# Sliding-window attention beside a gated feed-forward, one core: both heads of a pair in the two partition halves

## The chip, the cores and the metric

One core of one Trainium2 chip runs the kernel. The metric is the device time of an execution in microseconds (us), as the median of several executions; "span" is the length of the one execution that the profiler recorded, which is 1.6 to 1.8 us shorter than the time.

## The reference

The kernel computes one transformer layer: attention and a gated feed-forward from the same normalised input.

```python
# x: 1 x 2048 x 512;  32 heads of 16;  F = 1792
xn = layernorm(x)
q, k, v = split_heads(xn @ wqkv)
scores = q @ k.T * 16 ** -0.5            # per head
mask = (i - j >= 0) & (i - j < 256)      # causal, window of 256
o = softmax(where(mask, scores, -1e9)) @ v
out = x + o @ wo + ((xn @ w_gate) * (xn @ w_up)) @ w_down
```

## The kernel before

The 2048 tokens are four chunks (T) of 512 queries. The 32 heads are 16 pairs per token: a quarter c of the model's columns holds eight heads, four "even" ones (par 0) and four "odd" ones (par 1), and each of the four sits in its own block of 32 partitions (e). So there are 4 x 4 = 16 "pairs" (T, c), each of two "heads" (par) that really are four heads side by side. A head of 16 needs only a part of the matrix engine's 128 x 128 array, so the attention's matmuls are small tiles, and they are placed between the full-array matmuls of the feed-forward and the projections ("fillers"), whose order the program fixes beforehand.

A bank is here one 128 x 512 float32 tile of the memory that the matrix engine writes to: S has four, and four more (tag M) serve everything else in turn. In the profile's lines gp and up are the feed-forward's gate and up, psd is the sum of down and wo, acc that of the values, and OT the transposed attention output.

Scores come in batches of one four-bank tile S, one exponential each. The keys are on the partitions of the result. In the kernel before, an EVEN or ODD batch is of one par and puts the two 64-key halves of a key block into the two partition halves; a PLAIN batch holds what is left of both:

```python
def scores(self, T, c, kind, par):                      # 76 batches in all
    S = self.ps_s.tile([128, 4, 512], F32, tag="S")     # the one score tile
    for p, kb, h, q, n, col in self.score_pieces(T, kind, par):
        ...                                             # keys of one half, or of a block
        for e in range(4):
            nc.tensor.matmul(S[outs, e, col:col + n], lhsT=(Ko if p else K)[U][rows, c, keys],
                             rhs=Q[T][rows, c, q:q + n], tile_position=(32 * e, outs.start), ...)
    P = self.ppool.tile([128, 4, 512], BF16, tag="P")
    nc.scalar.activation(out=P[:], in_=S[:], func=ACT.Exp, scale=0.25)
    ...                                                 # POOL masks; DVE masks later
```

The value products contract over all 128 partitions. Where only one 64-key half of a block counts, they use copies of V with the other half zero (Vu, Vl), so half of the rows multiply zeros:

```python
def values(self, T, c, par):                            # 64 matmuls per head
    acc = self.ps_m.tile([128, 512], F32, tag="M")      # one of four banks, shared with the fillers
    for i, (P, col, h, kb, q, n) in enumerate(todo):
        V = self.V[U] if h == 2 else self.Vh[U % 2][h]  # whole, upper half or lower half
        for e in range(4):
            nc.tensor.matmul(acc[32 * e:32 * e + 32, q:q + n], lhsT=V[:, at:at + 32],
                             rhs=P[:, e, col:col + n], tile_position=(0, 32 * e), ...)
    nc.vector.transpose(out=at, in_=acc[:])             # then the reciprocal of the sums
    ...
def divide(self, T, c, par):                            # on = at * rz
    ...
    if par == 1:
        nc.vector.transpose(out=self.OT[T][:, c, :], in_=on)
```

The chain from values to OT: transpose, reciprocal, divide, transpose, all on VectorE (DVE). The output projection (wo) reads OT; its place among the fillers is:

```python
for b in range(4):                                      # after chunk T - 1, token tile b
    for g in todo.get(b, ()): add(*g)                   # the next norms
    down(T - 1, b)                                      # 14 matmuls
    wo(T - 1, b, (0, 1))
    wo(T - 1, b, (2, 3))                                # needs the OT of the last pair, c = 3
    add(0, lambda T=T, b=b: self.store(T - 1, b))
```

An eviction (the copy of a result out of its bank, which frees the bank) of a gate or of a query or key projection goes to ScalarE (ACT) instead of DVE when enough filler work has passed since the last score batch; the threshold is `ACT_FREE = 11`.

The softmax here doesn't subtract the row's maximum and nothing guards it: scores larger than these inputs give would overflow.

## Time and profile before

| | before |
|---|---|
| time, median (3 runs) | 274.67 us |
| span of the profiled run | 272.9 us |
| PE (matrix engine) busy | 263.3 us, 96% |
| DVE / ACT / POOL busy | 71% / 66% / 45% |
| score batch: first start to next full matmul | 0.36 us |
| values of one head (later chunks) | 0.80 us |
| values to OT, last step of a pair | 2.2 us |

The page of the kernel before: the busy times, and the engines of the chain of work that ended last.

```profile
PE 263.3 (96%) x4697; PEld 129.7 (48%) x4718; DVE 193.9 (71%) x376; ACT 178.9 (66%) x137; POOL 122.8 (45%) x293
...
PE 93%; ACT 4%; issue 1%; POOL 1%; DVE 0%; ACTq 0%
```

PE is what to shorten. (21 matmul records are missing from this trace: 4697 against 4718 weight loads. Sums of gaps have to allow for that.) The waits of PE, in us in total, number of times, longest:

```profile
PE wps L83 <- POOL ident L78: 1.4, 1, 1.4
PE S L276 <- ACT P L282: 0.8, 1, 0.8
```

The first is the start. The second is one score batch that waited for an exponential. No wait for a bank and none for OT is listed above 0.4 us. Next, PE's timeline around one score batch of 24 matmuls between full matmuls; the columns are start, us from the first start to the last modelled end, engine, line, operation, operands and count.

```profile
90.38 0.59 PE L366 MATMUL gp<-xnT,Wg 128*128 128x512 bf16 x2
90.90 0.43 PE L276 MATMUL S<-Q,Ko 32*64 32x64 bf16 x24
91.26 0.61 PE L366 MATMUL gp<-xnT,Wg 128*128 128x512 bf16 x2
```

The ends overlap and are modelled, so starts are what to read. A full matmul of 512 columns takes 0.216 us, so the two at 90.38 were through at 90.81; the batch starts 0.09 us later, and 0.36 us after its start the next full matmul starts. And PE's timeline over one head's values:

```profile
94.31 0.21 PE L335 MATMUL acc<-P,V 128*32 128x64 bf16 x4
...
94.86 0.32 PE L335 MATMUL acc<-P,V 128*32 128x64 bf16 x12
95.11 0.60 PE L380 MATMUL up<-xnT,Wu 128*128 128x512 bf16 x2
```

From 94.31 to 95.11 is 0.80 us. One place: the end of chunk 0's attention. The kernel before's PE and then DVE there (the entry in brackets is the idle time before, and what ended it):

```profile
69.20 0.59 PE L403 MATMUL psd<-Wo,OT 128*128 128x512 bf16 x2
70.58 0.29 PE L276 MATMUL S<-Q,K 16*128 16x128 bf16 x8 [0.78 <-ACT P L282]
...
70.91 0.64 PE L403 MATMUL psd<-Wo,OT 128*128 128x512 bf16 x2
```

```profile
68.89 0.72 DVE L340 STREAM_TRANSPOSE at<-acc 128x512 f32<-128x512 f32 x1 [1.41 <-PE acc L335]
...
70.39 0.71 DVE L356 STREAM_TRANSPOSE OT<-on 128x512 bf16<-128x512 bf16 x1
```

OT is ready at 70.39 + 0.71 = 71.10. The first of the two wo matmuls at 70.91 is of c = 2 and the second of c = 3, so the second, some 0.22 us later, finds OT just written. PE had itself been held for 0.8 us by the exponential, which is why.

### The profile page before, as it was taken

Reading aid. Unit: us, or ns where it says so; the run is one execution under the profiler, and the core shown is the slowest. Engines: PE = TensorE matmul, PEld = TensorE weight load, DVE = VectorE, ACT = ScalarE, POOL = GpSimd, SP = SyncE. Lnnn points to the kernel's source line nnn. Section 1 sums busy time; section 2 is a strip of 40 time slices with the busy share of each in tenths; the row PEclk is TensorE's granted clock in tenths of the full one; section 3 lists DMA queues with packets and bytes.
Section 4 is the critical chain, followed back from the end, with each engine's and each line's share of the span. In section 5 each row is a group of like instructions: output and inputs, shape, how many; then the busy total and the mean of one; then the engine's idle time right before and its main releaser. Section 6 shows DMA issues by size and latency. Waiting matters only on the chain.

```text
span 272.9 us, 10526 instructions
## 1 busy us (share of the span) xinstructions
PE 263.3 (96%) x4697; PEld 129.7 (48%) x4718; DVE 193.9 (71%) x376; ACT 178.9 (66%) x137; POOL 122.8 (45%) x293
## 2 busy tenths in 40 slices
PE   7999999999899999999999999999999999999993
PEld 6444444444444444444444444444544444444453
DVE  5398998878867678756976787684874568778331
ACT  8666687686556777688656667669866676665501
POOL 6135545465566242553646355253635425353500
PEclk9999999999999999999999999999999999999999
DMA  7999511100032100000022100000000000000002
GB/s 205 380 372 350 144 22 22 22 2 2 9 74 60 22 6 0 2 2 2 2 49 71 42 2 2 4 2 2 2 17 27 23 22 2 2 2 4 2 2 77
DMA packets 17181, 14.04 MB, mean 51 GB/s; under 512 B 7024, under 2 KB 17136, under 8 KB 17136
## 3 DMA queue, kind: packets, MB, share of 16 engines
q1 hardware_dynamic: 16848, 13.18, 15.9%
q8 instruction: 37, 0.61, 0.9%
q10 hardware_dynamic: 288, 0.20, 0.2%
q14 instruction: 8, 0.07, 0.1%
HBM read 9.70 MB, written 2.10 MB: 43 GB/s over the span
## 4 chain that ended last, share of the span: by engine, by line
PE 93%; ACT 4%; issue 1%; POOL 1%; DVE 0%; ACTq 0%
PE gp L366 19%; PE up L380 18%; PE psd L397 17%; PE qkp L206 10%; PE S L276 10%; PE acc L335 9%; PE vp L194 5%; PE psd L403 5%; ACT P L282 1%; ACT Vl L129 1%; ACT Vu L129 1%; ACT L75 0%; POOL P L290 0%; POOL P L294 0%; ACT xnT L181 0%
## 5 line engine op out<-in xcount | busy, mean ns | idle before, releaser
L282 ACT ACTIVATE P<-S 128x2048 bf16<-128x2048 f32 x76 | 142.7, 1877 | 59.7 <-PE S L276 40.1
L290 POOL TENSOR_SCALAR_AFFINE_SELECT P<-P 128x256 bf16<-128x256 bf16 x112 | 49.9, 466 | 124.3 <-ACT P L282 124.3
L366 PE MATMUL gp<-xnT,Wg 128*128 128x512 bf16 x224 | 59.7, 380 | 0.0
L380 PE MATMUL up<-xnT,Wu 128*128 128x512 bf16 x224 | 59.3, 380 | 0.0
L294 POOL TENSOR_SCALAR_AFFINE_SELECT P<-P 128x256 bf16<-128x256 bf16 x128 | 57.5, 472 | 0.0
L397 PE MATMUL psd<-Wd,hT 128*128 128x512 bf16 (+1 forms) x224 | 51.3, 366 | 1.8 <-issue 1.6
L384 DVE TENSOR_TENSOR hT<-up,gsb 128x512 bf16<-128x512 f32 x56 | 38.2, 682 | 14.3 <-PE up L380 13.5
L340 DVE STREAM_TRANSPOSE at<-acc 128x512 f32<-128x512 f32 x32 | 22.9, 716 | 23.4 <-PE acc L335 23.2
L305 DVE TENSOR_TENSOR P<-P,diag 128x512 bf16<-128x512 bf16 x64 | 31.4, 490 | 7.0 <-ACT P L282 6.9
L397 PEld LDWEIGHTS <-hT 128*128 128x128 bf16 x238 | 22.0, 98 | 23.2
L380 PEld LDWEIGHTS <-Wu 128*128 128x128 bf16 x224 | 20.4, 98 | 24.2
L366 PEld LDWEIGHTS <-Wg 128*128 128x128 bf16 x224 | 20.1, 98 | 23.5
L206 PE MATMUL qkp<-xnT,Wqkv 128*128 128x512 bf16 x128 | 30.0, 380 | 0.0
L335 PE MATMUL acc<-P,V 128*32 128x64 bf16 (+2 forms) x960 | 26.3, 221 | 0.0
L374 DVE CAST gsb<-gp 128x512 bf16<-128x512 f32 x33 | 22.4, 677 | 2.6 <-PE gp L366 1.8
L372 ACT ACTIVATE gsb<-gp 128x512 bf16<-128x512 f32 x23 | 13.7, 597 | 12.7 <-PE gp L366 12.7
L335 PE MATMUL acc<-P,Vu 128*32 128x64 bf16 x512 | 20.7, 193 | 0.0
L335 PEld LDWEIGHTS <-V 128*32 128x32 bf16 x960 | 17.9, 97 | 4.9 <-issue 0.4
L335 PE MATMUL acc<-P,Vl 128*32 128x64 bf16 x448 | 19.0, 193 | 0.0
L206 PEld LDWEIGHTS <-Wqkv 128*128 128x128 bf16 x128 | 11.6, 98 | 13.8
L276 PE MATMUL S<-Q,K 16*64 16x64 bf16 (+3 forms) x896 | 17.2, 236 | 0.9 <-ACT P L282 0.8
L276 PEld LDWEIGHTS <-K 16*64 16x64 bf16 (+1 forms) x896 | 8.3, 103 | 19.4 <-issue 19.4
(55 smaller groups left out, 244.5 us busy)
## 6 DMA issues: line engine op xcount, KB each, us to landing
Wg<-in_B_w_gate_dram SPq DMA_DIRECT2D x2, 896.0 KB, 10.2
Wu<-in_B_w_up_dram SPq DMA_DIRECT2D x2, 896.0 KB, 11.6
Wd<-in_B_w_down_dram SPq DMA_DIRECT2D x1, 1792.0 KB, 15.7
out_dram<-y SPq DMA_DIRECT2D x14, 128.0 KB, 1.7
Wqkv<-in_A_wqkv_dram SPq DMA_DIRECT2D x3, 512.0 KB, 5.9
x<-in_A_x_dram SPq DMA_DIRECT2D x1, 1024.0 KB, 10.4
x<-in_A_x_dram SPq DMA_DIRECT2D x1, 512.0 KB, 11.2
Wo<-in_A_wo_dram SPq DMA_DIRECT2D x1, 512.0 KB, 15.6
```

The costliest lines, as they stand in the source:

```text
L206: nc.tensor.matmul(ps[:], lhsT=self.Wqkv[:, k, lo:lo + 128], rhs=self.xnT[T][:, :, k, :], start=(k == 0), stop=(k == 3))
L276: nc.tensor.matmul(S[outs, e, col:col + n], lhsT=(self.Ko if p else self.K)[U][rows, c, keys], rhs=self.Q[T][rows, c, q:q + n], start=True ...
L282: nc.scalar.activation(out=P[:], in_=S[:], func=ACT.Exp, scale=0.25)
L290: nc.gpsimd.affine_select(out=P[:, :, col:col + 64], in_=P[:, :, col:col + 64], pattern=[[0, 4], [-1, 64]], compare_op=ALU.is_gt, fill=0.0 ...
L294: nc.gpsimd.affine_select(out=P[:, :, col:col + 64], in_=P[:, :, col:col + 64], pattern=[[0, 4], [1, 64]], compare_op=ALU.is_ge, fill=0.0, ...
L305: self.nc.vector.tensor_tensor(out=both, in0=both, op=ALU.min, in1=m.unsqueeze(1).to_broadcast([128, 4, 2, 64]))
L335: nc.tensor.matmul(acc[32 * e:32 * e + 32, q:q + n], lhsT=V[:, at:at + 32], rhs=P[:, e, col:col + n], start=(i == 0), stop=(i == len(todo) ...
L340: nc.vector.transpose(out=at.rearrange("p b r -> p (b r)"), in_=acc[:])
L366: nc.tensor.matmul(ps[:], lhsT=self.Wg[:, k, 128 * f:128 * f + 128], rhs=self.xnT[T][:, :, k, :], start=(k == 0), stop=(k == 3))
L380: nc.tensor.matmul(ps[:], lhsT=self.Wu[:, k, 128 * f:128 * f + 128], rhs=self.xnT[T][:, :, k, :], start=(k == 0), stop=(k == 3))
L384: nc.vector.tensor_tensor(out=self.hT[T][:, f, :], in0=ps[:], in1=self.gsb[:], op=ALU.mult)
L397: nc.tensor.matmul(ps, lhsT=self.hT[T][:, f, 128 * b:128 * b + 128], rhs=self.Wd[:, f, c0:c1], start=(f == 0), stop=False)
```

## The change

The intent: put the two heads of a pair, not two key halves of one head, into the two partition halves. A batch then holds the same keys and queries for both par. The value products contract over 64 rows, eight tiles of 64 x 32 at once (four blocks of 32 columns for par 0 in the upper rows, four for par 1 in the lower), with no zero rows. Each key half of V is needed in both partition halves, so a copy of V with the halves swapped (VS) is made by DMA. The core of the diff:

```diff
-        for p, kb, h, q, n, col in self.score_pieces(T, kind, par):
...
+        for m, q0, q1 in pieces:              # 2 or 3 pieces of 64 keys, 512 columns in all (four batches: 384)
+            for par in range(2):
+                for e in range(4):
+                    nc.tensor.matmul(S[64 * par:64 * par + 64, e, col:col + n],
+                                     lhsT=(self.Ko if par else self.K)[U][rows, c, keys],
+                                     rhs=self.Q[T][rows, c, q:q + n],
+                                     start=True, stop=True, tile_position=(32 * e, 64 * par),
...
-    def values(self, T, c, par):
-        acc = self.ps_m.tile([128, 512], F32, tag="M", name="acc")
+    def values(self, T, c, accs=None):
+            accs = [self.ps_m.tile([128, 512], F32, tag="M", name="acc") for _ in range(2)]
...
+            for par in range(2):
+                rows = slice(64 * par, 64 * par + 64)
+                for e in range(4):
...                                            # v: V where par is the key half, else VS
+                    nc.tensor.matmul(accs[par][32 * e:32 * e + 32, q:q + n], lhsT=v,
+                                     rhs=P[rows, e, col:col + n], ...,
+                                     tile_position=(64 * par, 32 * e), skip_group_check=True)
+        for par in range(2):
+            nc.vector.transpose(out=at[:, par].rearrange("p b r -> p (b r)"), in_=accs[par][:])
...                                            # divide: once per pair, twice the size
-    def zero_halves(self, j):                 # ACT and POOL zeroed Vu, Vl
-    def copy_halves(self, T):                 # DVE filled them
+    def swap_halves(self, T, queue):          # two DMAs per chunk
-        RESERVE = 38
+        RESERVE = 36
-        SCORES, VALUES = 1.85, 3.5
+        SCORES, VALUES = 1.85, 5.5
```

RESERVE, SCORES and VALUES are the weights by which the program spreads the fillers. Not shown, but part of the change too: one more buffer for P (7 instead of 6), and in the tail the last pair's values and the last sums take the four banks of S.

## The prediction

> What bounds it now. The matrix engine: 263.3 of 272.9 us busy (page, busy times), 93% of the chain that ended last. No wait of PE in the waits view is over 1.6 us in total. PE's timeline is a close sum: 197 us of full-array matmuls (512 columns every 0.216 us), about 62.6 us for the attention's small tiles, the rest start, tail and switches. ACT (66%), DVE (71%) and POOL (45%) matter only where PE needs a bank or OT.
>
> Small tiles, from PE's timeline. A batch of 24 score matmuls delays the full matmuls by 0.455 us: about 0.095 before its first start, 0.36 from its first start to the next full matmul. 512 columns per tile would be 0.213 us; a drain at each end and a bubble after short first pieces make the rest. A shared (PLAIN) batch takes 0.336. A head's 64 value matmuls take 0.80 us (0.63 in the first chunk), for 1536 columns = 0.64 us. The Trainium skill (TensorEngine Tiling, Tiling Modes) says that changing the mode drains the array and lists 64x32 as eight tiles; the switches of about 0.095 us in this trace agree.
>
> What changes.
> 1. Values: per pair 40 blocks of 64 columns in each half, both halves at once: 2560/2.4 = 1.07 us plus the overhead seen now (0.16) = 1.22, against 1.60; first chunk 0.96 against 1.26. 12 x 0.37 + 4 x 0.30 = 5.6 us saved. This assumes that two row halves accumulating in two banks overlap fully, as the scores' row tiles do now.
> 2. Scores: still 76 batches of 512 columns (four of 384), 16 or 24 matmuls. Longer first pieces hide the second weight load: estimate 0.32 to 0.34 instead of 0.36. About 1.8 us saved.
> 3. ACT's zeroing of Vu and Vl (2.13 + 2.14 us, in the chain) goes, but the first transposes are ready only some 0.4 us earlier: 0.3 us saved.
> 4. DVE: half copies (6.9 us) and 16 reciprocals go; the eight mask minima per pair become five ops of one or two blocks instead of four. POOL: still 16 selects per pair. Swaps: 8 DMAs, off the path. These are not critical.
> 5. New cost: the output chain after values. Now transpose 0.72, reciprocal 0.25, divide 0.43, OT transpose 0.71: 2.3 us after values. Then two transposes, one reciprocal, a divide of twice the size (estimate 0.70), one transpose: about 3.3 us. By the instruction order the output projection wants OT soon after the last pair of a chunk: chunk 0 about 1.3 us too early, chunk 1 about 1.0, the tail about 0.5. Loss 2.8 us. Banks: the two accumulators are waited for at their transposes, which are early enough.
>
> Sum: 274.7 - 5.6 - 1.8 - 0.3 + 2.8 = 269.8; I say 270.0, range 267.0 to 273.5. Faster by over 2%: 0.36; within 2%: 0.61; slower: 0.03.
>
> What would show it. (1) Values: 96 matmuls in about 1.2 us from the first to the next full matmul. (2) Score batches of 0.32 to 0.34 us. (3) First value projection 0.3 to 0.4 us earlier. (5) The waits view: PE or PEld on OT, about 1 us each at two chunk ends and in the tail. PE's full matmuls unchanged at 0.216 us.
>
> What would make it wrong. The two halves not overlapping, or eight weight loads per piece setting the pace: +5 to +17 us. Two transposes back to back delaying the evictions of gate and up, so that PE waits for banks after many pairs: +0.4 to 1 us per pair. ACT bound between 60 and 80 us (scores already waited 0.8 us for an exponential there): the saving there is not realised. Or fewer stalls than I count: 267.

## The result, and the profile after

| | before | after |
|---|---|---|
| time, median (range), 4 runs each | 274.71 us (274.65 to 274.87) | 273.38 us (273.19 to 273.49) |
| ratio, 95% interval | | 0.995, 0.9933 to 0.9967 |
| span of the profiled run | 272.9 us | 271.6 us |
| score batch of 512 columns, from first start to next full matmul | 0.36 us | 0.36 us |
| values of a pair, later chunks / first chunk | 1.59 / 1.25 us | 1.28 / 0.96 us |
| waits of PE for OT | none listed | 2.5 us, 3 times |

A ratio is the mean time of one kernel's fast runs over the mean of the other's fast runs of the same rounds, so it is not quite the ratio of the medians quoted. The forecast was 4.7 us of gain; 1.3 us came. The time lies within the range that was given, but the gain is less than a third of the one forecast.

The page after, the same two lines:

```profile
PE 261.7 (96%) x3886; PEld 120.2 (44%) x3886; DVE 182.3 (67%) x351; ACT 170.6 (63%) x131; POOL 113.4 (42%) x282
...
PE 86%; DVE 9%; DMA 2%; ACT 1%; SPq 0%; issue 0%; POOL 0%; DVEq 0%; POOLq 0%
```

DVE is now 9% of the chain that ended last, where it was 0%. The waits of PE say where:

```profile
PE psd L381 <- DVE OT L333: 2.5, 3, 1.5
PE wps L89 <- POOL ident L84: 1.4, 1, 1.4
PE S L258 <- ACT P L265: 0.5, 1, 0.5
PE acc L313 <- DVE hT L360: 0.5, 1, 0.5
```

Two of them are new: the output projection waits for OT, and the values wait for a bank. (The view counts idle time after the modelled end of the work before. Measured from start to start against the usual spacing, the three OT waits are 1.66, 0.89 and 0.49 us, 3.04 together, and the bank wait is 0.70. These larger figures are used below.) PE after around one score batch:

```profile
90.58 0.59 PE L342 MATMUL gp<-xnT,Wg 128*128 128x512 bf16 x2
91.11 0.22 PE L258 MATMUL S<-Q,K 16*64 16x64 bf16 x4
...
91.22 0.30 PE L258 MATMUL S<-Q,K 16*64 16x320 bf16 x4
...
91.47 0.61 PE L342 MATMUL gp<-xnT,Wg 128*128 128x512 bf16 x2
```

From 91.11 to 91.47 is 0.36 us, as before. And PE after over a pair's values, first and last lines of the sequence:

```profile
100.62 0.26 PE L313 MATMUL acc<-P,V 64*32 64x192 bf16 x4
100.63 0.26 PE L313 MATMUL acc<-P,VS 64*32 64x192 bf16 x4
...
101.67 0.29 PE L313 MATMUL acc<-P,VS 64*32 64x256 bf16 x4
101.90 0.60 PE L356 MATMUL up<-xnT,Wu 128*128 128x512 bf16 x2
```

From 100.62 to 101.90 is 1.28 us for 96 matmuls, against twice 0.80 before: the two row halves do overlap. The end of chunk 0's attention after, PE and then DVE:

```profile
69.42 0.25 PE L258 MATMUL S<-Q,K 16*64 16x128 bf16 x4 [0.51 <-ACT P L265]
...
69.78 0.39 PE L381 MATMUL psd<-Wo,OT 128*128 128x512 bf16 x1
71.66 0.39 PE L381 MATMUL psd<-Wo,OT 128*128 128x512 bf16 x1 [1.49 <-DVE OT L333]
```

```profile
68.41 1.31 DVE L319 STREAM_TRANSPOSE at<-acc 128x512 f32<-128x512 f32 x2 [1.77 <-PE acc L313]
...
70.89 0.71 DVE L333 STREAM_TRANSPOSE OT<-on 128x512 bf16<-128x512 bf16 x1
```

The chain is 68.41 to 71.60, 3.2 us instead of 2.2, and the wo matmul of c = 3 wants its result at about 70.0. It starts at 71.66. Finally the bank wait, PE and then DVE, after:

```profile
42.16 0.26 PE L313 MATMUL acc<-P,VS 64*32 64x192 bf16 x4
42.88 0.33 PE L313 MATMUL acc<-P,V 64*32 64x192 bf16 x8 [0.46 <-DVE hT L360]
```

```profile
41.01 0.42 DVE L286 TENSOR_TENSOR P<-P,diag 128x512 bf16<-128x512 bf16 x1
41.34 0.69 DVE L350 CAST gsb<-gp 128x512 bf16<-128x512 f32 x1
42.13 0.69 DVE L360 TENSOR_TENSOR hT<-up,gsb 128x512 bf16<-128x512 f32 x1
```

Values now take two of the four shared banks at once. The first half starts at 42.16; the second waits until DVE has emptied a bank of `up` at 42.82, the end of a row of DVE work in which no idle time is listed since 36.96.

### Where the time went, from the starts in PE's timeline

| term | forecast | measured in the two traces |
|---|---|---|
| values, 16 pairs | -5.6 | -4.9 (12 x 0.31 + 4 x 0.29) |
| scores, 76 batches | -1.8 | -0.1 |
| start, first score batch | -0.3 | -0.3 (13.98 to 13.69), in this pair of runs |
| waits for OT | +2.8 | +3.0 |
| bank wait of values | not in the sum | +0.7 |
| score waits | not in the sum | -0.1 (0.85 before; 0.58 and 0.14 after) |
| tail after the last matmul | not in the sum | +0.2 |
| sum | -4.9 | -1.5, against -1.25 of span |

The 0.1 us of the scores comes from the four batches of 384 columns (0.30 us each); the full ones took 0.356 us on average before and 0.358 after, since the 12 shared batches of 0.336 are gone. The sum leaves 0.2 us that these gaps don't place. It is an account, not yet a test: a stall that is taken away can uncover another. So the experiments.

### The profile page after: what moved, and what is told of

It is laid out like the page before. It is cut to its first block, busy times and chain, and to the rows that moved or that the text cites. A ratio compares the mean times of both kernels' runs of the same rounds, so it can differ in the third digit from the quotient of the medians.

```text
span 271.6 us, 8888 instructions
## 1 busy us (share of the span) xinstructions
PE 261.7 (96%) x3886; PEld 120.2 (44%) x3886; DVE 182.3 (67%) x351; ACT 170.6 (63%) x131; POOL 113.4 (42%) x282
## 3 DMA queue, kind: packets, MB, share of 16 engines
q1 hardware_dynamic: 18480, 14.06, 17.9%
## 4 chain that ended last, share of the span: by engine, by line
PE 86%; DVE 9%; DMA 2%; ACT 1%; SPq 0%; issue 0%; POOL 0%; DVEq 0%; POOLq 0%
PE gp L342 17%; PE up L356 17%; PE psd L375 16%; PE qkp L209 10%; PE S L258 9%; PE acc L313 6%; PE psd L381 4%; PE vp L197 4%; DVE at L319 2%; DMA Wqkv<-in_A_wqkv_dram 2%; DVE hT L360 1%; DVE OT L333 1%; DVE on L331 1%; PE L L375 1%; DVE gsb L350 1%; ACT P L265 1%
## 5 line engine op out<-in xcount | busy, mean ns | idle before, releaser
L137 POOL TENSOR_SCALAR_AFFINE_SELECT P<-P 64x256 bf16<-64x256 bf16 x224 | 96.8, 432 | 127.8 <-ACT P L265 117.2
L286 DVE TENSOR_TENSOR P<-P,diag 128x512 bf16<-128x512 bf16 (+1 forms) x76 | 30.6, 404 | 11.1 <-ACT P L265 11.1
L319 DVE STREAM_TRANSPOSE at<-acc 128x512 f32<-128x512 f32 x30 | 19.7, 695 | 19.3 <-PE acc L313 19.3
L258 PE MATMUL S<-Q,K 16*64 16x320 bf16 (+2 forms) x720 | 31.1, 260 | 0.6 <-ACT P L265 0.5
L258 PE MATMUL S<-Q,Ko 32*64 32x320 bf16 (+1 forms) x720 | 31.1, 260 | 0.0
L258 PEld LDWEIGHTS <-K 16*64 16x64 bf16 x720 | 12.3, 103 | 32.7 <-issue 32.7
L313 PE MATMUL acc<-P,VS 64*32 64x320 bf16 (+4 forms) x672 | 18.9, 254 | 0.0
L381 PE MATMUL psd<-Wo,OT 128*128 128x512 bf16 (+1 forms) x60 | 16.4, 374 | 2.5 <-DVE OT L333 2.5
L313 PE MATMUL acc<-P,V 64*32 64x320 bf16 (+4 forms) x672 | 18.4, 254 | 0.5 <-DVE hT L360 0.5
L399 DVE TENSOR_TENSOR y<-psd,x 128x512 bf16<-128x512 f32 x13 | 8.9, 688 | 13.3 <-PE psd L381 13.1
```

The costliest lines, as they stand in the source:

```text
L137: nc.gpsimd.affine_select(out=v, in_=v, pattern=pattern + [[1 if diag else -1, 64]], compare_op=ALU.is_ge if diag else ALU.is_gt, fill=0.0 ...
L258: nc.tensor.matmul(S[64 * par:64 * par + 64, e, col:col + n], lhsT=(self.Ko if par else self.K)[U][rows, c, keys], rhs=self.Q[T][rows, c, ...
L286: self.nc.vector.tensor_tensor(out=v, in0=v, op=ALU.min, in1=self.diag.unsqueeze(1).unsqueeze(1).to_broadcast([128, 4, n, 64]))
L313: nc.tensor.matmul(accs[par][32 * e:32 * e + 32, q:q + n], lhsT=v, rhs=P[rows, e, col:col + n], start=(i == 0), stop=(i == len(todo) - 1), ...
L381: self.nc.tensor.matmul(ps, lhsT=self.OT[T][:, c, 128 * b:128 * b + 128], rhs=self.Wo[:, c, c0:c1], start=False, stop=(c == 3))
```

## Experiments

All kernels compute the right result except where it is said. The theory: (a) the small-tile saving is real, about 5 us, and 3 us of it is lost because OT is late at the ends of chunks 0 and 1 and in the tail, 0.7 more by the bank wait; (b) a score batch costs its columns and its mode switch, whatever its pieces are. The rivals: the tiles themselves cost more than PE's starts show; the order of the fillers has nothing to do with it; the score bubble depends on the pieces.

### 1. The output projection later, in the changed kernel

The second token tile's `down` (14 matmuls, 3 us) is moved ahead of the first's second half of wo.

```diff
-                    for g in todo.get(b, ()):
-                        add(*g)
-                    down(T - 1, b)
+                    if b != 1:
+                        for g in todo.get(b, ()):
+                            add(*g)
+                        down(T - 1, b)
                     wo(T - 1, b, (0, 1))
+                    if b == 0:
+                        for g in todo.get(1, ()):
+                            add(*g)
+                        down(T - 1, 1)
                     wo(T - 1, b, (2, 3))
```

> Right kernel: the changed kernel with one edit in the order of the fill-in work: at the start of a chunk the down projection of the second token tile stands before the last half of the first tile's output projection, so that OT is wanted about 3 us later. Theory (the matrix engine stands still for OT because the output chain after the values has become 1 us longer, and that is on the critical path): the two stalls at the chunk ends (1.66 and 0.89 us between two output projections) go, the time falls by 2.0 to 2.6 us to about 271.0. Rival (ACT bounds that region, since a score batch waits for an exponential there in both kernels): PE then waits for exponentials instead, and the time falls by less than 0.8 us.

Measured, 5 rounds: 270.27 us (269.87 to 270.40), ratio 0.9833 (0.982 to 0.9845). That is 3.1 us less than the changed kernel's 273.38. The waits of PE and the place where the stall of 1.66 us was:

```profile
PE acc L313 <- DVE hT L360: 0.5, 1, 0.5
PE psd L381 <- DVE OT L333: 0.3, 1, 0.3
```

```profile
70.43 2.33 PE L375 MATMUL psd<-Wd,hT 128*128 128x512 bf16 x10
72.60 0.77 PE L381 MATMUL psd<-Wo,OT 128*128 128x512 bf16 x2
```

Ten `down` matmuls now stand between the score batch and wo. The OT waits of 1.66 and 0.89 us are gone but for 0.16, and so is the 0.58 us wait of a score batch for an exponential at that place: 2.4 + 0.6 = 3.0 us of stall for 3.1 us of time. The wait listed as 0.3 is the tail's, 0.49 from start to start. The bank wait stands as it was. So the OT stalls were truly on the path, and nothing else took their place.

### 2. The same edit in the kernel before (control)

> Right kernel, control: the kernel before with the same edit in the order of the fill-in work as e1. If e1's gain of 3.1 us came from the stalls for OT that the change brought in, the kernel before, whose output chain is 1 us shorter and which shows only one stall there (0.85 us, a score batch that waits for an exponential), gains less than 0.9 us: 273.8 to 274.7. If the edit is good for any order of work (rival), it gains 2 us or more here too.

Measured, 5 rounds: 273.86 us (273.79 to 274.48), ratio 0.9973 (0.9961 to 0.9985): 0.86 us gained. Its trace lists no wait of PE for the exponential any more; that wait was 0.85 us. So the edit isn't a gain that any version would get in full: the kernel before had only this one wait to lose. With the same order in both, the change is worth 273.86 - 270.27 = 3.6 us.

### 3. The two row halves one after the other

All 48 value matmuls of par 0 first, then the 48 of par 1.

```diff
-        for i, (P, col, m, q, n) in enumerate(todo):
-            ...
-            for par in range(2):
+        for par in range(2):
+            for i, (P, col, m, q, n) in enumerate(todo):
```

> Right kernel: all value products of one partition half first, then all of the other half; the same 96 matmuls. Theory (two row halves stream at the same time only because the order interleaves them; matmuls start in order): a pair's values take about 2 x 1.07 + 0.2 = 2.3 us instead of 1.28, and the time rises by 14 to 17 us to about 289. Rival (instructions, not columns, set the pace of the values): a pair's values stay within 0.1 us of 1.28 and the time within 2 us of 273.4.

Measured, one look: 280.95 us. A pair's values take 1.92 us: neither the theory's 2.3 nor 1.28. PE's timeline of one pair's values shows why not 2.3:

```profile
102.31 0.40 PE L313 MATMUL acc<-P,V 64*32 64x192 bf16 x8
102.54 0.61 PE L313 MATMUL acc<-P,VS 64*32 64x192 bf16 x20
102.98 0.26 PE L313 MATMUL acc<-P,V 64*32 64x64 bf16 x8
103.03 0.26 PE L313 MATMUL acc<-P,VS 64*32 64x192 bf16 x4
103.06 0.31 PE L313 MATMUL acc<-P,V 64*32 64x320 bf16 x4
```

In the program par 0's pieces are V 192 and 320 columns, then VS (five pieces, 20 matmuls), then V 64, 128 and 320, then VS and V 256. Par 1 starts with VS 192 columns. The four VS matmuls at 103.03 are par 1's first piece. They start before par 0's V of 320 columns at 103.06, which stands ahead of them in the program, and 0.72 us after par 0 began. The trace has this in all 16 pairs, each time over the last 12 matmuls of par 0. So PE brought a later matmul of the other row half forward by itself, but only when no more than 12 matmuls were left in between. The Trainium skill ("TensorE: Matmul & The Clock Gate", Part 3, The mechanism) says that matmuls "are pc-monotone in start AND end — strict FIFO, no reordering". For tiles in different row halves this trace disagrees about the starts, and the measurement decides. The same section lets weight loads for another row group go ahead through a window of 64 entries; the trace shows a matmul going ahead, too. For the prediction: alternating the halves in the program, as the change does, is worth 0.64 us per pair (0.50 in the first chunk) over leaving it to the engine.

### 4. Narrow pieces first in the values

The question was whether the order of a pair's pieces causes the excess of the values over their columns (1.28 against 1.07 us for 2560 columns at 2.4 per ns; that rate is the trace's: the next piece starts 0.136 us after one of 320 columns and 0.056 us after one of 128, so 192 columns take 0.080 us).

```diff
+        todo.sort(key=lambda w: w[4])
```

> Right kernel: the value pieces of a pair sorted by width, 64 columns first, 320 last. In the changed kernel the starts of a piece's eight matmuls spread over 0.024 us until about the 60th matmul and over 0.058 us after it. Theory (the supply of instructions falls short at a narrow piece late in the run, and the lag then stays to the end): with wide pieces last the spread stays near 0.03, a pair's values take 1.23 to 1.25 us instead of 1.28, and the time falls by 0.4 to 0.8 us. Rival (the spread comes with the count of matmuls, whatever their width): unchanged, 1.27 to 1.29, time within 0.2 us.

Measured, 5 rounds: 274.13 us (273.02 to 275.30), ratio 0.9965 (0.9945 to 0.9986); values 1.31 us per pair. Both theories missed. It is slightly worse per pair. The spread of a piece's eight starts, 0.023 us at first, reaches 0.058 to 0.070 us as early as the 30th matmul here, and not before about the 60th in the order of the change. Why the spread grows was not settled. The time itself scatters more than in other kernels, and the runs with a granted clock (the share of full speed that the profile reports for PE) of 0.993 or 0.994 are the slow ones: 274.67 to 275.30 us, against 273.02 to 273.58 at 0.999 or 1.0. The profile, which is of a slow one, shows where it lost the time. A row of its view by stretches, with the granted clock as the last figure but two:

```profile
71.73:75.14 3.41, 3.15 (x8) 1.19 (x9) 2.64 (x7) 0.41 (x1) 2.04 (x6) 0.50 0.13 41
```

From the end of the stall for OT after chunk 0 on (the wo matmul that waited starts at 72.00), the clock is at one half until 75.14, and full matmuls start 0.427 us apart in place of 0.216. The eight full matmuls up to 75.27 took 3.27 us where 1.73 is usual: 1.5 us lost, about the distance between the two groups. Whether the stall brings it about was not tested; the changed kernel has the same stall, and its four runs have clocks of 0.999 or 1.0. The values of 1.31 us lie outside that stretch. At the full clock the time is that of the changed kernel (273.19 to 273.49), so this run says nothing finer about the time than "not better".

### 5. Score batches of one piece

Every batch one piece of 512 columns, 8 matmuls. Its output is wrong, which doesn't matter for the time. The work of the other engines and the columns are the same.

```diff
-        for m, q0, q1 in pieces:
-            ...
+        col = sum(64 * (q1 - q0 + 1) for m, q0, q1 in pieces)
+        U, j = divmod(8 * T + pieces[-1][0], 8)
```

> Wrong result on purpose: each score batch is one piece of 512 columns (384 in one batch), eight matmuls instead of 16 or 24, with keys of one block only; P has the same size. Theory A (what a batch costs beyond its columns is fixed: drains of 0.095 at both ends, a spread of 0.023, and a bubble of 0.027 that belongs to the second piece's weight load): without a second piece 0.33 us from first start to the next full matmul instead of 0.357, and 76 x 0.027 = 2 us less in total. Theory B (the bubble belongs to the start after a switch, not to a second piece): 0.357 as now, time within 0.5 us of the changed kernel. My prediction's idea (longer first pieces hide the load) had 0.32 to 0.34 for the kernel as it is.

Measured, one look: 273.45 us; the result is wrong, as meant. PE's timeline around one batch:

```profile
91.38 0.41 PE L258 MATMUL S<-Q,K 16*64 16x512 bf16 x4
91.39 0.41 PE L258 MATMUL S<-Q,Ko 32*64 32x512 bf16 x4
91.73 0.60 PE L341 MATMUL gp<-xnT,Wg 128*128 128x512 bf16 x2
```

From 91.38 to 91.73 is 0.35 us (0.354 as the median), against 0.357 with two pieces and 0.362 with three. A single piece with no second weight load costs almost the same. The prediction's step 2 is refuted here: the bubble that it meant to hide behind longer pieces isn't tied to the pieces. What remains beyond 0.213 us of columns is a fixed 0.14 us: 0.093 of switch back to the full array, 0.023 of spread between the eight starts, and about 0.025 more, close to the 0.027 that stands between the first and the second piece, whatever the first piece's width (64, 128, 192 and 256 columns were all seen).

### 6. The tail

As experiment 1, and three more units of filler work between the last pair's `divide` and the last wo.

```diff
-        fill(spent + 12, -1)
+        fill(spent + 15, -1)
```

> Right kernel: e1, and in the tail 15 instead of 12 units of fill-in work between the last values and the last output projections. Theory: the stall of 0.49 us for OT there is on the path to the end; it goes and the time falls by 0.4 to 0.5 us against e1, to about 269.8. Rival: the end is set by the last stores, which the edit does not move earlier: within 0.1 us of e1.

Measured, 5 rounds: 269.80 us (269.59 to 270.43), ratio 0.9825 (0.9812 to 0.9838), 0.47 us less than experiment 1. The tail's OT wait of 0.49 us is gone from the trace. The ranges of the two overlap, so the size is a likely one only; that the wait went is plain.

### 7. ACT's zeroing put back

Experiment 1 with two activations that write zeros at the start, which nobody reads; 3.83 us where the kernel before had 4.27.

```diff
+        for rows in (slice(64, 128), slice(0, 64)):
+            nc.scalar.activation(out=Z[rows].rearrange("p e x -> p (e x)"),
+                                 in_=zero[rows].to_broadcast([64, 2048]), func=ACT.Copy)
```

> Right kernel: e1, and ACT writes zeros to two halves of a strip buffer at the start (2 x 64x2048, about 1.9 us each), as it did for Vu and Vl before. My prediction gave the removal of the zeroing 0.3 us: then this costs 0.2 to 0.4 us against e1. Rival 1 (the chain that ended last had the two fills with 1.6% of the span): about 4 us. Rival 2 (the start is set by the norms of the four tiles on DVE and POOL, so ACT's early work is worth nothing): under 0.1 us.

Measured, 5 rounds: 269.95 us (269.77 to 272.70), ratio 0.9847 (0.9817 to 0.9877), against 270.27 without the zeroing. No cost shows. ACT is through with it at about 6.1 us (2.31 + 3.83), and its first eviction of transposes is recorded at 6.04, against 6.55 in experiment 1 and 6.02 in the changed kernel, both without zeroing, and 6.49 in the kernel before. The zeroing put back is 0.44 us shorter than the old one, so this isn't an exact undoing; but the first score batch itself starts anywhere from 13.63 to 14.49 us in the profiled runs of kernels with the same start (13.71 here, 14.06 in experiment 1), so the 0.3 us of step 3 is not more than that scatter. The times alone can't tell so small a cost: in this profile the bank wait at 42 us is 0.30 us and not 0.70.

### 8. More evictions on ACT: ACT_FREE 9, with the tail edit

```diff
-ACT_FREE = 11
+ACT_FREE = 9
```

> Right kernel: e5, and the threshold from which a gate eviction goes to ACT lowered from 11 to 9 units after the scores, so that fewer fall to DVE. In chunk 0 the chain of the changed kernel runs on DVE from 29 to 43 us and ends in a wait of the values for a bank (0.70 us at 42 us). Theory (DVE is late in chunk 0): the wait gets shorter or goes, 0.3 to 0.7 us less than e5. Rival (exponentials are delayed by the evictions in front of them and the scores wait): no gain or a loss.

Measured, 5 rounds: 268.90 us (268.56 to 269.11), ratio 0.9787 (0.9775 to 0.9800). 0.90 us less than experiment 6. The values at the place of the bank wait:

```profile
42.21 0.26 PE L313 MATMUL acc<-P,VS 64*32 64x192 bf16 x4
42.27 0.34 PE L313 MATMUL acc<-P,V 64*32 64x192 bf16 x8
```

The second half starts 0.06 us after the first, not 0.72. The wait of 0.70 us is gone (the 0.2 us that the time gained beyond it is within the scatter of the two kernels), and DVE's work in the whole kernel has fallen from 182.1 to 170.6 us.

### 9. Both edits in the kernel before (second control)

The kernel before with the later output projection and ACT_FREE 9.

> The fair control for the best version so far: the kernel before with the same two edits (output projection of the first token tile later, ACT_FREE 9), at 268.90 us with the change. My theory: the kernel before has no wait of PE for a bank that the threshold could cure (its accounting has one stall, 0.845 us, and the order edit already removed it), so the threshold is worth under 0.3 us here and this run is 273.6 to 274.1 us. Rival: sending more evictions to ACT helps any version of this kernel by about 0.9 us; then 272.8 to 273.2 us, and the gain of ACT_FREE 9 belongs to no stall of the change.

Measured, 5 rounds: 273.73 us (273.66 to 274.03), ratio 0.9965 (0.9953 to 0.9977). The threshold is worth 0.1 us here, against 0.9 us in the changed kernel: the bank wait belongs to the change. On equal footing the change is worth 273.73 - 268.90 = 4.8 us (with the tail edit, which only the changed kernel needs). The traces give the same: PE's small tiles with their waits take 58.4 us in experiment 2, whose trace lacks one record, and 53.6 us in experiment 8, which lacks none: 4.8.

### 10. ACT_FREE 9 alone

The changed kernel with the threshold and nothing else.

> The changed kernel with ACT_FREE 9 alone (the output projection as early as it was). Theory: the values' 0.70 us wait at 42 us goes, the two waits for OT at the chunk ends (1.66 and 0.89 us) and the tail's 0.49 us stay: 272.4 to 272.8 us against 273.38. Rival: with a less loaded DVE the OT chain at the chunk ends comes sooner too, and the waits for OT shrink by half or more: under 271.8 us.

Measured, 5 rounds: 273.20 us (272.01 to 274.31, granted clocks 0.994 to 1.0), ratio 0.9941 (0.9916 to 0.9966). The waits of PE:

```profile
PE psd L381 <- DVE OT L333: 2.5, 3, 1.5
...
PE S L258 <- ACT P L265: 0.8, 1, 0.8
```

The bank wait is no longer listed, and the OT waits stand unchanged, against the rival. The wait for an exponential before the first OT stall grew from 0.58 to 0.85 us, so part of the gain was taken up there. The median is above the forecast of the theory; the three runs with a clock of 0.999 or 1.0 were at 272.01 to 272.52, the three at 0.994 at 273.88 to 274.31. The two groups lie 1.7 us apart, about as in experiment 4, where the trace showed a stretch at half clock; no trace of a run at 0.994 was kept here. Against the changed kernel's four runs, all at 0.999 or 1.0, the three fast ones are 0.7 to 1.5 us shorter. The time fits the theory no better than that.

### 11. ACT_FREE 7

> The best version with ACT_FREE 7 in place of 9. Theory: no wait of PE over 0.2 us is left for it to cure (the 268.90 us version shows only start-up waits and 0.17 us on OT), so it is within 0.3 us of 268.90 us if ACT still has room. Rival: more evictions on ACT delay the next batch's exponential and with it the scores: PE waits for P, over 269.4 us.

Measured, 5 rounds: 268.66 us (268.56 to 269.06), ratio 0.978 (0.9768 to 0.9793): the same as experiment 8, as expected with no wait left to cure. This or ACT_FREE 9 is the version to keep: correct, and 6 us below the kernel before.

## Why the prediction was right or wrong

1. **Values: right in mechanism, 0.7 us too big.** "2560/2.4 = 1.07 us plus the overhead seen now (0.16) = 1.22" came out as 1.28 in the later chunks, while the first chunk's 0.96 was exact. The term that was mis-sized is the overhead. Before, a piece's four starts were spread over 0.010 us and 0.099 us of switch followed. After, the last piece's eight starts are spread over 0.058 us (0.033 in the first chunk) and 0.095 us of switch follows. The rest of the excess, 0.06 us in sum (0.05 before), lies between the pieces. The excess is thus 0.21, not 0.16; 12 pairs x 0.06 = 0.7. The assumption of overlap held, and experiment 3 shows that the alternation in the program is what gives it.
2. **Scores: wrong, 1.7 of 1.8 us missing.** This is the step that failed: "Longer first pieces hide the second weight load: estimate 0.32 to 0.34 instead of 0.36." The batch kept 0.36, and experiment 5 shows 0.354 with no second piece at all. The extra time is a fixed toll of the batch, but for some 0.004 us per piece. The shared batches of 0.34 that the prediction compared with have four tiles at a time where the others have eight. In the trace of the kernel before, their four starts spread over 0.010 us in place of 0.023, and their first piece costs 0.014 us beyond its columns in place of 0.027; gaps of 0.003 to 0.007 between the later pieces take some of it back. So they were cheaper by another shape of tile, which the new batches don't have.
3. **Zeroing: about 0.** The first value projection did come earlier, 7.12 to 6.85 us in the two profiles, but putting a zeroing back costs nothing that can be measured (experiment 7). The saving was counted from a chain of waits in one execution, at a place whose scatter is larger: without zeroing the first value projection starts between 6.69 and 7.64 us in the profiles.
4. **DVE, POOL and DMA not critical: right for POOL and DMA, wrong for DVE in one place.** The DMA of VS is never in PE's waits. DVE's dense row at 37 to 43 us cost the 0.70 us bank wait.
5. **Output chain: right; its sentence on banks was wrong.** 3.2 us against 3.3 forecast; stalls of 1.66, 0.89 and 0.49 against 1.3, 1.0 and 0.5. Experiments 1 and 6 take them away and get their time back. But "the two accumulators are waited for at their transposes, which are early enough" failed once: the second accumulator waited 0.70 us for a bank before its values could start.

Waits for banks were named among the things that would make the prediction wrong ("0.4 to 1 us per pair"), but by another road (transposes delaying the evictions after a pair), and left out of the sum. What came struck one pair of 16, before its values. So three steps failed, by size: the score saving of step 2 (1.7 us), the overhead of the values in step 1 (0.7) and the banks of step 5 (0.7). The experiments leave little open in the balance: 0.7 (values) + 1.7 (scores) + 0.2 (OT) + 0.7 (bank) = 3.3 of the 3.4 us between 4.7 and 1.3; the 0.3 us at the start and the tail's 0.2 are of the size of the unplaced rest. Where the gain went, then: of about 5 us that the tiles save, 3.6 us net (3.0 + 0.7 - 0.1) were turned into new waits for DVE, and these were recoverable by order (experiments 1 and 6) and by moving evictions (experiment 8). What is not settled: why the spread of starts grows within a pair's values, and why the pieces sorted by width do worse.

The skill's page "TensorEngine Tiling (Array Packing)", Tiling Modes, Key Properties, says that changing the mode drains the engine. The traces fit that and give the price, 0.09 to 0.10 us on each side of a batch. It could have warned me off step 2, since a drain for the mode has nothing to do with the number of pieces.

## What to carry to other kernels

When small tiles are packed tighter, what they feed moves too: list the consumer of every lengthened chain, compare its place in the program with the new end of the chain, and change the order in the same edit. A fixed toll per batch does not fall with fewer pieces (with fewer batches it should, which was not tested here), and one kernel with one piece tells which it is. And give a change its control: the same side edits in the old kernel showed that 4.8 us of the 5.8 belong to the change.

## What the Trainium skill lacked or had wrong

- "TensorE: Matmul & The Clock Gate", Part 3, The mechanism: matmuls are said to start strictly in program order. With 64-row tiles of two row halves, a matmul of the other half started before one that stands 12 ahead of it in the program (103.03 against 103.06 us in experiment 3), and two blocks of 48 took 1.92 us per pair where interleaved ones took 1.28. Order in the program still matters.
- The same page, Measured speedup vs the span model: about 4 ns per further tile. The traces agree where it is fresh: eight starts in 0.023 us (3.3 ns each), four in 0.010. Later in a long row of eight-tile pieces it is 0.058 (8.3 ns each), which the page doesn't mention.
- "TensorEngine Tiling (Array Packing)", Key Properties: that a mode switch drains is said, but not what it costs. Here it was 0.091 to 0.099 us at each change of tile shape, and about 0.025 us more once per score batch of eight tiles, for a first piece of any width from 64 to 512 columns.
